# Weight blocks of a transformer layer fetched by several smaller DMAs instead of one

## The chip, the cores and the metric

The kernel runs on one core of a Trainium2 chip. The metric is device time in microseconds (us) from the start to the end of one execution; lower is better. Three executions of the kernel before the change took 1088.27, 1091.22 and 1091.68 us, so the median is 1091.22 us. Another execution was recorded by the hardware profiler: it took 1091.97 us, of which the span from the first to the last instruction is 1090.2 us.

Names used below: TensorE (PE in the profile, with its weight loads as PEld) multiplies matrices, ScalarE (ACT) applies functions, VectorE (DVE) does elementwise work, GpSimd (POOL) a few small operations, and SyncE (SP) issues every DMA of this kernel. SBUF is the on-chip memory, with 128 partitions; PSUM takes the results of TensorE; HBM is the main memory, where inputs, weights and output lie.

## What is computed

One pre-norm transformer layer on a sequence of 2048 rows with 1024 features, in bf16: attention with 32 heads of 32 features, then a feed-forward block with 3584 hidden units.

```python
x = A_x                                       # (1, 2048, 1024)
q, k, v = split(layernorm(x) @ A_wqkv)        # (1024, 3072), 32 heads of 32
p = softmax(q @ k.T * 32**-0.5)               # per head, 2048 x 2048
h = x + concat(p @ v) @ A_wo                  # (1024, 1024)
g = gelu(layernorm(h) @ B_w1 + B_b1)          # (1024, 3584)
out = h + g @ B_w2 + B_b2                     # (3584, 1024)
```

The weights don't fit into the SBUF beside the attention's data, so the weights of the second half (`A_wo`, `B_w1`, `B_w2`, and part of `A_wqkv`) are fetched again for every stretch of 256 rows.

## The kernel before

**Work.** The 2048 rows are cut into eight units of 256 rows. For each unit and each group of four heads, attention makes scores on TensorE (`Att.qk`, matmuls at line 784), takes their exponentials on ScalarE (line 795, tiles `PT` of 128 x 1024), multiplies them with V on TensorE (`Job.pv`, line 821) and sums them with a matmul against ones (`Job.den`, line 850, after a pairwise addition on VectorE at line 836). Between these, as TensorE work of lower priority, come the projection and feed-forward matmuls, made by `mm` (lines 539 to 554): line 546 is a matmul split over four column tiles, lines 549 and 552 the same matmul whole.

**Loops.** After the keys, values and the first queries are made, the loop at line 1133 runs over the units u = 0 to 5: output projection of the next unit (`wo`, line 902), half of the second feed-forward matmul (`ffn2`, line 987), the norm (`ln2`, line 930), the other half of `ffn2`, the first feed-forward matmul of the next unit (`ffn1`, line 943), and the attention of unit u + 3. Units 6 and 7 follow in a tail.

**Weight blocks.** `ffn1` needs 14 blocks of `B_w1` for a unit, `wo` needs 4 blocks of `A_wo`, and `late_q` (line 691) fetches blocks of `A_wqkv` for the later queries. All of these come from `wblock` (line 897): a block is 1024 rows x 256 columns, 512 KB, laid down as 128 partitions with eight runs of 512 bytes each. They go around a ring of four buffers `a_w1r` (line 484), and for the last unit through fourteen buffers `b_w1r` (line 489). `ffn2` needs seven blocks of `B_w2` for each half of a unit (line 994): 512 rows x 512 columns, also 512 KB, as 128 partitions with four runs of 1 KB. Their ring `a_w2r` has seven buffers, and `b_w2r` seven more for the end. Each block was one DMA, hence one instruction on SP, at line 570 inside `dma`.

**Order.** The kernel is written as a graph of tasks (`Graph`). `schedule` (line 109) plays the graph through once at build time with assumed durations and so fixes the order of the instructions on each engine. For a DMA it assumes that SP is taken for `dma_issue` = 0.06 us, that bytes flow at 280 GB/s one DMA behind the other, and a fixed latency (lines 178 to 191). Its result is only an order: on the chip every engine runs its own list in that order, and waits where a semaphore tells it to. A DMA task belongs to one of 24 lanes, each with a semaphore of its own; a DMA adds 16 to it when it has landed, and who needs the data waits for the total that `assign` (line 242) works out. A new task on a lane waits for the one before. SP also waits, before it issues a block, until the matmuls that read the old block in that buffer are done; everything behind it in SP's list waits too. That list also holds the loads of queries (`QT`), residual rows (`hch`), the transposes of the normed rows (`hnT`, line 575) and the stores of the output.

**Emission.** `emit` (line 318) writes for each task its waits, its instructions (`t.fns`, a list) and one semaphore increment on the last of them.

Of the kernel before, what the change touches and what calls it, by code (L numbers as in the profile page):

```python
# [10 lines left out]
E = mybir.EngineType  # L11

P = 128
# [47 lines left out]
class Graph:  # L61
# [47 lines left out]
    def schedule(self, pick_pe, pool, switch=0.104, dma_rate=280.0, dma_lat=2.1, dma_issue=0.06):  # L109
# [5 lines left out]
        free = {e: 0.0 for e in self.ENGS}  # L115
# [5 lines left out]
        n = 0  # L121
# [19 lines left out]
        while n < total:  # L141
            if not events:
                raise RuntimeError("schedule: stuck")
            now = heapq.heappop(events)
            while events and events[0] <= now + 1e-9:
                heapq.heappop(events)
            for e in self.ENGS:
                while free[e] <= now + 1e-9:
                    up = upcoming[e]
                    rd = ready[e]  # L150
                    while up and up[0][0] <= now + 1e-9:
                        rd.append(heapq.heappop(up)[2])
                    if not rd:
                        break
                    if e == E.PE:
                        t = pick_pe(rd, now, state, free_banks(now))
                    else:
                        t = min(rd, key=lambda x: (x.prio, num[x]))
                        if up and t.prio > 0:

                            for (rt, _, u) in up[:6]:
                                if u.prio < t.prio and rt < now + 0.6 * t.occ:
                                    t = None
                                    break
                    if t is None:
                        break
                    rd.remove(t)
                    if t.acq is not None:
                        b = min([x for x in free_banks(now) if x in t.acq.banks], key=lambda x: max([y.done for y in pool[x]], default=0.0))
                        t.deps.update(pool[b])  # L170
                        t.acq.n = b
                        pool[b] = t.acq
                    start = now
                    if e == E.PE:
                        if state["mode"] != t.mode:
                            start += switch
                        state["mode"] = t.mode
                    t.order = len(seqs[e])
                    seqs[e].append(t)
                    if e == E.SP:  # L180
                        k = min(range(self.n_lanes), key=lambda i: lanes[i].done if lanes[i] else 0.0)
                        if lanes[k] is not None:
                            t.deps.add(lanes[k])
                            start = max(start, lanes[k].done)
                        lanes[k] = t
                        t.lane = k
                        free[e] = start + dma_issue
                        s0 = max(state["dma"], start + 0.9)
                        state["dma"] = s0 + t.bytes / dma_rate / 1e3
                        t.done = max(state["dma"], s0) + dma_lat - 0.9  # L190
                    else:
                        free[e] = start + t.occ
                        t.done = start + t.occ + t.lat
                    if t.rel is not None:
                        t.rel.rel.append(t)
                        if len(t.rel.rel) == t.rel.nrel:
                            pool[t.rel.n] = t.rel.rel
                        heapq.heappush(events, t.done)
                    heapq.heappush(events, free[e])
                    n += 1  # L200
                    for s in t.succ:
                        s.left -= 1
                        if s.left == 0:
                            release(s)
# [20 lines left out]
    def assign(self, flows, lane_flows):  # L225

        for t in self.tasks:
            best = {}
            keep = set()
            for d in t.deps:  # L230
                if d.eng == E.SP:
                    keep.add(d)
                elif d.eng != t.eng or t.eng != E.PE:
                    b = best.get(d.eng)
                    if b is None or d.order > b.order:
                        best[d.eng] = d
            t.deps = keep | set(best.values())
            for d in t.deps:
                d.inc = True
        lane_n = [0] * len(lane_flows)  # L240
        for e in self.ENGS:
            c = 0
            for t in self.seqs[e]:
                if e == E.SP:
                    lane_n[t.lane] += 1
                    t.inc = True
                    t.flow = ("L", t.lane)
                    t.value = 16 * lane_n[t.lane]
                else:
                    t.flow = ("E", e)  # L250
                    if t.inc:
                        c += 1
                    t.value = c

        clock = {}
        topo = self._topo()
        last = {}
        for t in topo:
            e = t.eng
            prev = last.get(e)  # L260
            base = dict(prev) if prev else {}
            waits = {}
            for d in t.deps:
                if base.get(d.flow, 0) >= d.value:
                    continue
                if waits.get(d.flow, (0, None))[0] < d.value:
                    waits[d.flow] = (d.value, d)

            keep = dict(waits)
            for f, (v, d) in waits.items():  # L270
                for g, (v2, d2) in waits.items():
                    if g != f and g in keep and clock[d2].get(f, 0) >= v:
                        keep.pop(f, None)
                        break
            t.waits = [(f, v) for f, (v, d) in keep.items()]
            for f, (v, d) in waits.items():
                for k, x in clock[d].items():
                    if base.get(k, 0) < x:
                        base[k] = x
                if base.get(f, 0) < v:  # L280
                    base[f] = v
            last[e] = base
            if t.inc:
                c = dict(base)
                if e != E.SP:
                    c[t.flow] = t.value
                else:
                    c[t.flow] = t.value
                clock[t] = c
        self.sems = {}  # L290
        for e, s in flows.items():
            self.sems[("E", e)] = s
        for i, s in enumerate(lane_flows):
            self.sems[("L", i)] = s
# [23 lines left out]
    def emit(self, e, obj):  # L318
        for t in self.seqs[e]:
            for f, v in t.waits:  # L320
                obj.wait_ge(self.sems[f], v)
            ins = None
            for fn in t.fns:
                ins = fn(obj)
            if t.inc:
                ins.then_inc(self.sems[t.flow], 16 if e == E.SP else 1)


def build_kernel(nc, A_x, A_wqkv, A_wo, B_w1, B_b1, B_w2, B_b2, out):
# [7 lines left out]
    DC = D // P  # L337
# [9 lines left out]
    gr = Graph(N_LANES)  # L347
# [217 lines left out]
    def dma(out_ap, in_ap, nbytes, reads=(), writes=(), prio=0, noncontig=False, after=()):  # L565
        def fn(s):
            if noncontig:
                with nc.allow_non_contiguous_dma(reason="strided gather"):
                    return s.dma_start(out_ap, in_ap)
            return s.dma_start(out_ap, in_ap)  # L570
        return gr.add(E.SP, fn, 0.06, 0.0, reads, writes, prio, nbytes=nbytes, after=after)


    def dma_transpose(out_ap, in_ap, nbytes, reads, writes, prio):
# [5 lines left out]
         reads=[B_ident], writes=[B_ident])  # L580
# [315 lines left out]

    def wblock(R, src_ap, prio=1):
        s = R.next("w1", R.nw1)
        dma(R.w1[:, s, :, :], src_ap.rearrange("(dc p) c -> p dc c", p=P), P * DC * 512, writes=[R.B_w1[s]], prio=prio)
        return s  # L900

    def wo(u, tail=False):
# [84 lines left out]
    def ffn2(u, j, wide=False, W=None, banks=None):  # L987
        R = R2 if wide else R1
        W = W or R1
        c = slice(512 * j, 512 * j + 512)  # L990
        ws = []
        for q in range(FC // 4):
            s = W.next("w2", W.nw2)
            dma(W.w2[:, s, :, :], B_w2[512 * q:512 * q + 512, c].rearrange("(f p) c -> p f c", p=P),
                P * 4096, writes=[W.B_w2[s]], prio=1)
            ws.append(s)
        for t in range(2):
            bank = banks[t] if banks and banks[t] is not None else slot()
# [3 lines left out]
            for fc in range(FC):  # L1002
                s = ws[fc // 4]
# [20 lines left out]
    for k in range(80):  # L1024
        pe(lambda p: p.matmul(psum[:, 6, 0:256], ident[:, :], b2t[:, 0:256], start=True, stop=True), 0.18 if k < 42 else 0.115,  # L1025
           reads=[B_ident, B_b2t], writes=[B_ps[6]], kind="warm")
# [21 lines left out]
    for hc in range(8):  # L1048
# [6 lines left out]
        for k, r in [(k, hc) for k in range(min(hc, NLJ))] + ([(hc, r) for r in range(hc + 1)] if hc < NLJ else []):  # L1055
            n = 8 * k + r
            s = NR + 15 if n == 0 else n - 1 if n < 9 else n
# [220 lines left out]
```

## Time and profile before

| what | value |
|---|---|
| median of three runs | 1091.22 us (1088.27 to 1091.68) |
| profiled execution, of which span | 1091.97 us, 1090.2 us |
| TensorE busy, weight loads beside it | 1045.6 us, 609.6 us |
| ScalarE, VectorE, GpSimd busy | 1014.5, 755.9, 43.4 us |
| mean granted TensorE clock | 0.994 |
| 16 DMA engines, mean over the span | 54.1% for the kernel's own queue, 163 GB/s |
| DMAs: `a_w2r`, `a_w1r` (B_w1), `a_w1r` (A_wo), `b_w1r`, `a_w1r` (A_wqkv), `b_w2r` | 105, 98, 32, 14, 11 and 7 of 512 KB |
| median from issue to landing, in that order | 5.7, 4.4, 4.2, 6.1, 5.0 and 6.6 us |

How to read it: a busy share says how much of the time an engine had an instruction in hand, so two engines over 90% leave little that can be gained by moving work. The DMA share counts the time that packets took on the 16 DMA engines, and the time to landing counts from SP's issue to the last semaphore update. SP itself isn't in the list of busy engines: its instructions issue or wait.

### The profile page before, as it was taken

What the parts mean: (1) busy time and instruction counts of PE and PEld (TensorE: products, weight loads), DVE (VectorE), ACT (ScalarE), POOL (GpSimd) and SP (SyncE); (2) the same over time, 40 slices, a digit from 0 to 9 for tenths busy, and PEclk for the clock granted to TensorE, in tenths of its full rate; (3) what the DMA queues carried; (4) which work ended last, traced back from release to release, by engine and by line L of the source; (5) the groups of instructions that cost most, each with busy time, mean ns of one, the idle gap of its engine ahead of it and who ended that gap; (6) DMA issues with size and microseconds to landing.
All of it is one profiled execution on the core that took longest, in us unless ns stands there. A gap on an engine that the chain in (4) does not pass through costs nothing.

```text
span 1090.2 us, 41817 instructions
## 1 busy us (share of the span) xinstructions
PE 1045.6 (96%) x19048; PEld 609.6 (56%) x19107; DVE 755.9 (69%) x1453; ACT 1014.5 (93%) x1116; POOL 43.4 (4%) x110
## 2 busy tenths in 40 slices
PE   8989999998899999999999999999999999999998
PEld 6656555554344664574475457446545754474483
DVE  7886666666576896599489659948974967696401
ACT  4989999999999999999999999999999999999650
POOL 3200000000010001001000100100010000000100
PEclk9999999999999999999999999999999999899999
DMA  7640010008464667665685766567586656987370
GB/s 194 199 123 11 14 41 3 2 3 287 142 167 133 183 180 209 210 189 154 209 251 157 220 215 189 155 217 233 142 239 205 182 179 160 308 236 228 96 246 20
DMA packets 280146, 178.03 MB, mean 163 GB/s; under 512 B 42656, under 2 KB 274976, under 8 KB 279200
## 3 DMA queue, kind: packets, MB, share of 16 engines
q1 hardware_dynamic: 279968, 175.35, 54.1%
q8 instruction: 150, 2.46, 0.9%
q14 instruction: 28, 0.23, 0.1%
HBM read 161.16 MB, written 10.49 MB: 157 GB/s over the span
## 4 chain that ended last, share of the span: by engine, by line
PE 54%; ACT 39%; DVE 5%; issue 1%; DMA 1%; SPq 0%; POOL 0%; POOLq 0%; DVEq 0%
ACT PT L795 35%; PE ps L549 18%; PE ps L546 12%; PE ps L784 8%; PE ps L821 6%; PE ps L552 5%; PE ps L850 3%; ACT PX L795 2%; DVE PS L836 2%; ACT uu L983 2%; DMA xrb<-in_A_x_dram 0%; DVE OD L866 0%; PE ps L1025 0%; SPq L570 0%; DVE OD L873 0%
## 5 line engine op out<-in xcount | busy, mean ns | idle before, releaser
L795 ACT ACTIVATE PT<-ps 128x1024 bf16<-128x1024 f32 x992 | 922.4, 1082 | 14.7 <-PE ps L784 14.3
L836 DVE TENSOR_TENSOR PS<-PT 128x1024 bf16<-128x1024 bf16 x434 | 286.6, 685 | 128.9 <-PE ps L850 68.1
L784 PE MATMUL ps<-QT,KT 32*128 32x256 bf16 x4096 | 205.3, 274 | 10.7 <-ACT PT L795 5.4
L821 PE MATMUL ps<-PT,V 128*32 128x256 bf16 x3968 | 174.4, 274 | 2.8 <-ACT PT L795 2.8
L784 PEld LDWEIGHTS ps<-QT,KT 32*128 32x128 bf16 x4096 | 61.2, 92 | 166.3 <-ACT PT L795 134.8
L850 PE MATMUL ps<-PS,ones 128*32 128x256 bf16 x1792 | 124.6, 275 | 4.8 <-DVE PS L836 4.0
L821 PEld LDWEIGHTS ps<-PT,V 128*32 128x32 bf16 x3968 | 102.1, 97 | 29.4 <-issue 6.8
L549 PE MATMUL ps<-hnT,a_w1r 128*128 128x256 bf16 x949 | 116.5, 274 | 1.1 <-DVE gT L961 0.5
L549 PEld LDWEIGHTS ps<-hnT,a_w1r 128*128 128x128 bf16 x949 | 87.9, 98 | 25.8 <-issue 14.5
L546 PE MATMUL ps<-a_w2r,gT 128*32 128x512 bf16 x1372 | 98.3, 381 | 0.4 <-DVE hch L1007 0.2
L549 PE MATMUL ps<-a_w2r,gT 128*128 128x512 bf16 x382 | 93.8, 380 | 4.2 <-issue 2.9
L546 PE MATMUL ps<-hnT,a_w1r 128*32 128x256 bf16 x2476 | 88.9, 274 | 4.0 <-issue 1.6
L961 DVE TENSOR_TENSOR gT<-ps,b1f 128x512 bf16<-128x512 f32 x98 | 67.2, 686 | 17.5 <-PE ps L546 9.3
L546 PEld LDWEIGHTS ps<-hnT,a_w1r 128*32 128x32 bf16 x2476 | 60.4, 96 | 20.6 <-issue 16.8
L1007 DVE SCALAR_TENSOR_TENSOR hch<-ps,hch 128x512 bf16<-128x512 f32 x32 | 21.9, 685 | 69.9 <-PE ps L552 47.1
L850 PEld LDWEIGHTS ps<-PS,ones 128*32 128x32 bf16 x1792 | 47.0, 96 | 30.7 <-DVE PS L836 14.2
L549 PEld LDWEIGHTS ps<-a_w2r,gT 128*128 128x128 bf16 x413 | 35.2, 98 | 47.4 <-issue 13.4
L549 PE MATMUL ps<-xnT,Wall 128*128 128x512 bf16 (+1 forms) x256 | 53.5, 344 | 4.5 <-DVE rr L876 2.8
L983 ACT ACTIVATE uu<-uu 128x1024 bf16<-128x1024 bf16 x49 | 53.9, 1108 | 0.0
L546 PEld LDWEIGHTS ps<-a_w2r,gT 128*32 128x32 bf16 x1372 | 30.0, 96 | 25.6 <-issue 14.0
L603 POOL CAST mvb<-mv 128x2 bf16<-128x2 f32 (+1 forms) x25 | 4.9, 201 | 987.2 <-DVE mv L600 987.2
L549 PE MATMUL ps<-Wall,xnT 128*128 128x128 bf16 (+1 forms) x443 | 43.9, 247 | 0.0
(89 smaller groups left out, 1007.9 us busy)
## 6 DMA issues: line engine op xcount, KB each, us to landing
a_w2r<-in_B_w_dram SPq DMA_DIRECT2D x105, 512.0 KB, 5.7
a_w1r<-in_B_w_dram SPq DMA_DIRECT2D x98, 512.0 KB, 4.4
a_w1r<-in_A_wo_dram SPq DMA_DIRECT2D x32, 512.0 KB, 4.2
b_w1r<-in_B_w_dram SPq DMA_DIRECT2D x14, 512.0 KB, 6.1
a_w1r<-in_A_wqkv_dram SPq DMA_DIRECT2D x11, 512.0 KB, 5.0
Wall<-in_A_wqkv_dram SPq DMA_DIRECT2D x17, 256.0 KB, 4.7
xrb<-in_A_x_dram SPq DMA_DIRECT2D x16, 256.0 KB, 4.0
hch<-in_A_x_dram SPq DMA_DIRECT2D x16, 256.0 KB, 5.2
```

The costliest lines, as they stand in the source:

```text
L546: fns.append(lambda p, j=j: p.matmul(psum[32 * j:32 * j + 32, bi(bank), c0:c1], lhsT[:, 32 * j:32 * j + 32], rhs, start=start, stop=stop, ...
L549: t.whole = lambda p: p.matmul(psum[:, bi(bank), c0:c1], lhsT, rhs, start=start, stop=stop, skip_group_check=True)
L552: t = pe(lambda p: p.matmul(psum[:, bi(bank), c0:c1], lhsT, rhs, start=start, stop=stop), occ, reads=reads, writes=[bb(bank)], mode="full" ...
L603: pool(lambda g: g.tensor_copy(mvb[:, sl, :], mv_l[:, sl, :]), 0.25, reads=B_mv[sl], writes=B_mvb[sl], prio=prio)
L784: return p.matmul(psum[:, 2 * us[h // 2] + h % 2, 256 * i:256 * i + 256], KT[32 * h:32 * h + 32, g, k0:k0 + P], QT[32 * h:32 * h + 32, qs, :],
L795: act(lambda a, u=u, k=k: a.activation(PTs[s][:, k, :, :], psum[:, 2 * u:2 * u + 2, :], ACT.Exp, bias=0.0, scale=SCALE), 1024, reads=[B_ps ...
L821: fns.append(lambda p, i=i, h=h: p.matmul(psum[32 * h:32 * h + 32, bi(bank), 0:256], V[:, g, 2 * r + i, 32 * h:32 * h + 32], PTs[s][:, h / ...
L836: dve(lambda v: v.tensor_tensor(PS[:, n, :, :], pairs[:, :, 0:256], pairs[:, :, 256:512], ALU.add), c_dve(1024, 2), reads=B_PTs[s], writes ...
L850: fns.append(lambda p, h=h, rhs=rhs, i=i: p.matmul(psum[32 * h:32 * h + 32, bi(bank), 256:512], ones32[:, :], rhs, start=False, stop=last, ...
L961: t = dve(lambda v: v.tensor_tensor(g[:, fc:fc + 2, :], psum[:, bi(bank), :].rearrange("p (f c) -> p f c", f=2), b1f[:, fc:fc + 2].unsquee ...
L983: act(lambda a: a.activation(w, w, ACT.Tanh, bias=0.0, scale=KT2), 1024, reads=[B_uu[i]], writes=[B_uu[i]], prio=-1)
L1007: drop(dve(lambda v, hs=hs, bank=bank, half=half: v.scalar_tensor_tensor(hch[:, hs, c], psum[:, bi(bank), :], half, hch[:, hs, c], ALU.mul ...
```

## The change

A weight block is now fetched by several DMAs that each cover some of the partitions: four of 32 partitions for the blocks of `wblock` (`B_w1`, `A_wo`, late `A_wqkv`), two of 64 partitions for the blocks of `B_w2`. The pieces of one block are one task of the graph, with one list of waits ahead of the first piece; each piece adds 16 to the same lane's semaphore, so a reader waits for 64 or 32 more than before the block instead of 16 more. The bytes, the length of the runs and the buffers stay as they were. The planner counts SP as taken for 0.06 us for every piece; its bytes and latency are unchanged. All other DMAs stay single.

```diff
@@ schedule
-                        free[e] = start + dma_issue
+                        free[e] = start + dma_issue * len(t.fns)
@@ assign
-                    lane_n[t.lane] += 1
+                    lane_n[t.lane] += len(t.fns)
@@ emit
             for fn in t.fns:
                 ins = fn(obj)
+                if e == E.SP and fn is not t.fns[-1]:
+                    ins.then_inc(self.sems[t.flow], 16)
             if t.inc:
                 ins.then_inc(self.sems[t.flow], 16 if e == E.SP else 1)
@@ build_kernel
+    def dma_pieces(piece, nbytes, n, reads=(), writes=(), prio=0):
+        w = P // n
+        fns = [lambda s, a=a: s.dma_start(*piece(slice(a, a + w))) for a in range(0, P, w)]
+        return gr.add(E.SP, fns, 0.06 * n, 0.0, reads, writes, prio, nbytes=nbytes)
@@ wblock
-        dma(R.w1[:, s, :, :], src_ap.rearrange("(dc p) c -> p dc c", p=P), P * DC * 512, writes=[R.B_w1[s]], prio=prio)
+        src = src_ap.rearrange("(dc p) c -> p dc c", p=P)
+        dma_pieces(lambda q: (R.w1[q, s, :, :], src[q]), P * DC * 512, 4, writes=[R.B_w1[s]], prio=prio)
@@ ffn2
-            dma(W.w2[:, s, :, :], B_w2[512 * q:512 * q + 512, c].rearrange("(f p) c -> p f c", p=P),
-                P * 4096, writes=[W.B_w2[s]], prio=1)
+            src = B_w2[512 * q:512 * q + 512, c].rearrange("(f p) c -> p f c", p=P)
+            dma_pieces(lambda z, s=s, src=src: (W.w2[z, s, :, :], src[z]), P * 4096, 2, writes=[W.B_w2[s]], prio=1)
```

## The prediction

> **What bounds the kernel.** I read the page's busy times first, then the chain that ended last, then the engines' timelines wherever the chain says "issue", and last the DMA views.
>
> ```profile
> PE 1045.6 (96%) x19048; PEld 609.6 (56%) x19107; DVE 755.9 (69%) x1453; ACT 1014.5 (93%) x1116; POOL 43.4 (4%) x110
> ...
> PE 54%; ACT 39%; DVE 5%; issue 1%; DMA 1%; SPq 0%; POOL 0%; POOLq 0%; DVEq 0%
> ...
> L795 ACT ACTIVATE PT<-ps 128x1024 bf16<-128x1024 f32 x992 | 922.4, 1082 | 14.7 <-PE ps L784 14.3
> ```
>
> ScalarE's exponentials and TensorE bound the kernel together; DMA is 1% of the chain, and that lies in the lead. From about 77 to 1020 us ScalarE is the fuller: its whole idle time there is about 8 us. A shorter time to landing can thus bring almost nothing by itself. I paired every weight block's landing with the first weight load that reads it: one late `A_wqkv` block (302.28 us) is met after 0.06 us, one `A_wo` block after 0.84, all 265 others after 1.2 us or more, the typical `B_w1` block after 4 to 5. Weights aren't waited for. What else do the DMAs hold up? The chain near 433 us, and ScalarE's timeline there:
>
> ```profile
> 432.75 0.32 PE ps L784 x5
> 433.08 1.23 issue
> 434.31 0.31 PE ps L784 x3
> ```
>
> ```profile
> 434.64 5.62 ACT L795 ACTIVATE PT<-ps 128x1024 bf16<-128x1024 f32 x6 [1.46 <-PE ps L784]
> ```
>
> TensorE stops for 1.23 us in the midst of eight score matmuls that belong to one task, with nothing to wait for, and ScalarE loses 1.46 us. I followed what could starve it: the instructions themselves.
>
> ```profile
> q1 hardware_dynamic: 279968, 175.35, 54.1%
> q8 instruction: 150, 2.46, 0.9%
> ```
>
> Queue 8 moves 150 packets of 2.46 MB / 150 = 16 KB. TensorE's stream has 19,107 weight loads, as many matmuls and 180 others, 38,394 in all, and 38,394 / 150 = 256: each packet is 256 TensorE instructions. In the records of single packets, six stalls of TensorE without a releaser begin exactly 449 or 450 instructions after 256 times the number of packets that had landed, and end 1.3 to 1.6 us after the next packet's end: 433.08 (1.23 us), 588.64 (0.52), 746.08 (0.60), 764.05 (0.45), 815.83 (1.49) and 863.86 (0.41), 4.70 us together. The ScalarE gaps that follow are 1.46, 0.69, 0.51, 0.73, 1.47 and 0.61, 5.47 us together. So TensorE runs out of instructions.
>
> **Why the fetch is late.** Where DMA is idle (100 to 250 us), the packets start 0.5 to 1.5 us after TensorE passes instruction 168 of its block, the spot that makes this delay most even; I take it as the request. Among weight DMAs the delay is 1 to 4.6 us. It ends at DMA boundaries: with one `a_w1r` block under way the packet starts 0.06 to 0.8 us before that block's landing (2.62 against 2.84 us after the request; 1.97 against 2.39; 1.48 against 1.69). In bursts of `a_w2r` it lets two go by: request at 427.31, blocks landing 2.86, 4.20 and 6.57 us later, packet at 4.56; request at 810.52, blocks at 1.38, 3.66 and 5.00, packet at 4.35. The fetch waits for the rest of the DMA in hand and the whole of the next, not for all queued bytes.
>
> [...]
>
> **The change, part by part.**
>
> *The fetch's wait.* A `B_w1` block gives each of 16 DMA engines 64 packets of 512 B at 27 ns, 1.7 us; a quarter is 0.43 us. A `B_w2` block gives 32 of 1 KB at 46 ns, 1.5 us; a half is 0.74. The wait of up to two DMAs falls from 3.0 to 3.4 us to 0.9 to 1.5 us. The stalls at 433 and 815.83 lie in `B_w2` bursts: the packet comes some 1.5 us earlier, against stalls of 1.23 and 1.49; the other four stalls are under 0.6. I take all six as gone: -4.7 us. Bounds: -5.5 by ScalarE's gaps, 0 if the fetch doesn't profit. What is late next is ScalarE itself: its only other gaps over 0.2 us there (1.03 at 275.8, 0.43 at 291.9, 0.36 at 945.2) end on attention work that the change leaves alone.
>
> *SP's time.* Added are 3 x 155 + 112 = 577 issues, each with its semaphore update.
>
> ```profile
> L570 SPq DMA_DIRECT2D a_w2r<-in_B_w_dram x105: 367/368/2237, 134.5 to 1038.3; - x105
> L570 SPq DMA_DIRECT2D a_w1r<-in_B_w_dram x98: 367/368/1467, 340.3 to 973.0; - x98
> ```
>
> An issue takes 0.37 us; 256 KB loads issued back to back in the lead take 0.43 plus 0.04 between. Four pieces are 0.37 + 3 x 0.47 = 1.8 us, two are 0.84, so SP gains about 577 x 0.47 = 271 us on the 228 it issues now; it mostly waits for buffers. In dense `ffn1` blocks are issued every 2.2 us (359.51, 361.69), in `B_w2` bursts every 1.3 us (421.46, 422.79, 424.04): it fits both. Queued behind the pieces are `QT` loads, used 50 us or more after landing save one before 100 us, and `hnT`, below.
>
> *Landing.* The last quarter is issued 1.4 us after the first. A 64 KB load lands 1.7 to 1.9 us after issue, a 256 KB one 2.6 at best; 128 KB should take about 2.1. That gives 3.5 us against 3.45 to 3.9 for an undivided block alone. Bounds: 0.6 earlier, or 1.4 later if a piece takes as long to land as a block. I take 0, the nearer rows being those of smaller loads; cover is the slack above.
>
> *The crowded stretch.* At 919 to 946 us the DMA engines are full:
>
> ```profile
> 919.00:946.00 27.00, 24.95 (x465) 11.61 (x458) 17.41 (x34) 26.59 (x30) 1.53 (x4) 0.87 1.07 317
> ```
>
> The second `hnT` transpose is issued there at 933.10, 3.3 us after its data were ready, and used 3.43 us after landing. Ahead of it since 919.7 are six blocks of four pieces and four of two: 6 x 1.4 + 4 x 0.47 = 10.3 us more issue time. SP already stands blocked there (issues of 1.67 and 2.24 us), so most of it replaces blocking: I take 0, bound 10.3 - 3.43 = 6.9 us.
>
> *Plan and waits.* No wait is added: a block's waits stand ahead of its first piece as before. In the planner only back-to-back issues shift, by 0.06 to 0.18 us; I take 0.
>
> **Sum.** 1091.97 - 4.7 = 1087.3 for the profiled execution. It lay 0.75 above the median, so for the median 1091.22 - 4.7 = **1086.5**, own range 1083 to 1089.
>
> **Rivals.**
>
> *No gain: 1091.2.* The fetch waits for a fixed number of bytes or packets already queued, whatever DMA they belong to. For: the six stalls all have queued blocks. Waits that end after one `a_w1r` (64 packets on an engine) or two `a_w2r` (also 64) fit this as well. Against: at 972.54 a packet waits past two `a_w1r`-sized blocks (landings at 1.57 and 3.83, packet at 3.90), and the starts sit at boundaries.
>
> *SP late: 1095.* If landings move by the full 1.4 us, the blocks at 302.28, 290.26 and 780.36 (1.27 us of slack) stall for 1.34 + 0.56 + 0.13 = 2.0 us, and `hnT` costs its 6.9: 1086.5 + 8.9 = 1095.4. Against: SP's blocking above.
>
> *Slower pieces: 1120.* This is the case on the other side: a piece that covers a quarter or half of the partitions may move slower than its share. No DMA of this trace covers fewer than 128 partitions, so the factor f is bounded by 1 (a piece takes its share of the time) and 2 (a half takes as long as a whole). Place: the dense `ffn1` phases, where a block is used every 2.2 us; queued `a_w1r` blocks land every 1.5 us (965.2 to 971.3), `a_w2r` every 1.3. It decides from f = 2.2 / 1.5 = 1.47. Above, each of six units loses 18 x (1.5 f - 2.2) + 7 x 1.3 x (f - 1), less some 3.5 of slack: at f = 1.6 5.6 us, six times 34 us, 1086.5 + 34 = 1120; at 2, 120 us. For: the crowded stretch shows that DMA can become the bound. Against: 33% of DMA time is free at 300 to 980 us.
>
> [...]
>
> *It doesn't do what it says:* the waits count all pieces, so this could only be the planner reordering; it is inside "no gain".
>
> **Chances.** Forecast 0.53, no gain 0.17, SP late 0.13, slower pieces 0.17. The last is left out of the range, which runs from 1082.5 to 1100 (SP late with no gain). A difference under 0.3% (3.3 us) can't be told from none here. Faster by more: 0.47 (the forecast up to 1087.9); within: 0.25 (the rest of it 0.06, no gain 0.17, 0.02 of SP late); slower: 0.28 (SP late 0.11, slower pieces 0.17).
>
> **What would show it.** Right: the stalls at instruction 449 vanish, fetch packets start within 2.5 us of the request, SP issues about 1,000 DMAs, landings stay near 4 to 6 us. Wrong: DMA share above 67% at 300 to 980 us or packets longer than 27 and 46 ns (slower pieces); weight loads waiting for `a_w1r` or `hnT` (SP late); the same six stalls (no gain).

## The result and the profile after

The change makes the kernel slower: 1123.87 us (median of six runs, 1121.27 to 1125.26) against 1091.44 us for the kernel before (median of six, 1088.27 to 1097.06). The ratio is 1.0293, 95% interval 1.0264 to 1.0323, or 32.4 us. The profiled execution took 1125.26 us, its span 1123.5 us. One of the five executions of the run e10 below took 1986.44 us, for a reason that no record shows, and is left out of that run's ratio.

The page of the kernel after: busy times, the kernel's own DMA queue, the chain, ScalarE's exponentials (busy us, mean ns of one, idle us ahead of them), and two DMA rows (count, KB each, us to landing).

```profile
PE 1055.2 (94%) x19048; PEld 611.9 (54%) x19107; DVE 756.5 (67%) x1453; ACT 1017.6 (91%) x1116; POOL 43.5 (4%) x110
...
q1 hardware_dynamic: 289200, 175.38, 64.7%
...
PE 55%; ACT 29%; DVE 6%; DMA 5%; issue 3%; SPq 2%; POOL 1%; POOLq 0%; DVEq 0%
...
L804 ACT ACTIVATE PT<-ps 128x1024 bf16<-128x1024 f32 x992 | 923.5, 1070 | 48.1 <-PE ps L793 47.2
...
a_w2r<-in_B_w_dram SPq DMA_DIRECT2D x210, 256.0 KB, 6.2
a_w1r<-in_B_w_dram SPq DMA_DIRECT2D x392, 128.0 KB, 3.0
```

ScalarE does the same work, but its exponentials now stand idle for 48.1 us where it was 14.7, waiting for scores. So it is TensorE that falls behind. The same bytes keep the DMA engines busy for 64.7% of the span, 54.1% before, although only 3% more packets move (289,200 against 279,968). The packets themselves take longer: in the packet records the ones of 1 KB (mostly `B_w2` blocks) take 69.5 ns on average and were at 49.4; those of 512 B (mostly blocks of `wblock`) 32.6 and were at 28.3. In the stretch of the units, TensorE's busy time, its weight loads, VectorE, ScalarE, GpSimd, the clock, the DMA share and GB/s, first of the kernel before, then after:

```profile
300.00:980.00 680.00, 660.75 (x12658) 382.35 (x12689) 517.63 (x995) 673.97 (x732) 22.23 (x56) 0.99 0.67 197
```

```profile
300.00:980.00 680.00, 643.44 (x12102) 366.00 (x12136) 493.67 (x947) 651.84 (x705) 22.30 (x56) 0.98 0.77 185
```

More DMA time (0.77 against 0.67) for fewer bytes in a second (185 against 197 GB/s): this is a slower transfer, not more traffic. What TensorE waits for, total us, times and longest:

```profile
PE ps L548 <- issue: 9.7, 6, 3.1
PE ps L551 <- issue: 9.2, 33, 3.7
PE ps L793 <- issue: 6.2, 4, 2.5
...
PE ps L548 <- DMA a_w1r<-in_B_w_dram: 3.9, 2, 2.4
...
PE ps L551 <- DMA a_w2r<-in_B_w_dram: 2.5, 4, 0.8
```

Two kinds of wait are there. The first is "issue", a stop with nothing to wait for. (Of the 9.2 us in the second row, 3.7 are the wait for `hnT` told below; of the rest, most are short ones, of which the kernel before has 4.6 us in 28.) The chain of waits at 761 us shows the longest, and ScalarE's timeline what it loses there:

```profile
760.58 0.44 PE ps L548 x12
761.02 3.09 issue
764.12 0.41 PE ps L548 x3
```

```profile
766.83 1.02 ACT L804 ACTIVATE PT<-ps 128x1024 bf16<-128x1024 f32 x1 [4.17 <-PE ps L793]
```

Counted as in the prediction (stops that begin at instruction 449 or 450 after the last fetched packet, over 0.2 us), there are 12 of 17.1 us together after and 7 of 4.95 us before (the prediction's six and one of 0.25). The second kind is new, a wait for weights. Here the chain at 534 to 543 us:

```profile
533.98 8.30 DMA a_w2r<-in_B_w_dram
542.29 0.05 issue
542.33 1.04 PE ps L551 x4
```

A half whose issue starts at 533.98 lands 8.3 us later, and a matmul of `ffn2` waits for it. Ten of 105 `B_w2` blocks now land less than 0.3 us before they are used, none before the change. The waits for weights (3.9 + 2.5 + 0.4 us), one of 3.66 us for the transposed rows `hnT` at 965.33 and one of 1.48 at 323.94 (VectorE, which has to free a PSUM bank first, waits for a store of late queries that stands behind pieces in SP's list) make 11.9 us. Only 2.9 of them are for `B_w2` blocks. A third share can't be separated: TensorE's clock was granted at half for 34.1 us of the span, 13.7 before, in pieces of 3.4 us of which several follow a stop (at 664.9 after the one at 662.1; at 763.8 and 866.2, as the ones from 761.0 and 864.1 end). If all of that lay on the path it cost up to 10 us. The sum, 12.1 + 11.9 + at most 10, is about the 32.4 measured, but it is no proof, since parts can overlap. ScalarE's gaps over 0.2 us from 80 us on grew in step, from 7.3 to 38.9 us.

### The profile page after: what moved, and what is told of

Same layout as the page of the kernel before. It is cut to its first block, busy times and chain, and to the rows that moved or that the text cites. A ratio compares the mean times of both kernels' runs of the same rounds, so it can differ in the third digit from the quotient of the medians.

```text
span 1123.5 us, 42394 instructions
## 1 busy us (share of the span) xinstructions
PE 1055.2 (94%) x19048; PEld 611.9 (54%) x19107; DVE 756.5 (67%) x1453; ACT 1017.6 (91%) x1116; POOL 43.5 (4%) x110
## 3 DMA queue, kind: packets, MB, share of 16 engines
q1 hardware_dynamic: 289200, 175.38, 64.7%
q8 instruction: 150, 2.46, 0.9%
## 4 chain that ended last, share of the span: by engine, by line
PE 55%; ACT 29%; DVE 6%; DMA 5%; issue 3%; SPq 2%; POOL 1%; POOLq 0%; DVEq 0%
ACT PT L804 25%; PE ps L551 19%; PE ps L548 13%; PE ps L793 9%; PE ps L830 6%; PE ps L554 5%; PE ps L859 4%; ACT PX L804 2%; DMA a_w2r<-in_B_w_dram 2%; SPq L579 2%; DVE PS L845 2%; ACT uu L993 1%; DMA a_w1r<-in_B_w_dram 1%; DMA q_scratch<-lq 1%; DVE st L607 1%
## 5 line engine op out<-in xcount | busy, mean ns | idle before, releaser
L804 ACT ACTIVATE PT<-ps 128x1024 bf16<-128x1024 f32 x992 | 923.5, 1070 | 48.1 <-PE ps L793 47.2
L793 PE MATMUL ps<-QT,KT 32*128 32x256 bf16 x4096 | 206.3, 275 | 13.7 <-issue 6.2
L548 PE MATMUL ps<-hnT,a_w1r 128*32 128x256 bf16 x2476 | 91.9, 279 | 14.9 <-issue 9.1
L859 PEld LDWEIGHTS ps<-PS,ones 128*32 128x32 bf16 x1792 | 47.8, 97 | 31.9 <-DVE PS L845 13.8
L551 PE MATMUL ps<-xnT,Wall 128*128 128x512 bf16 (+1 forms) x256 | 54.7, 349 | 4.7 <-DVE rr L885 3.0
```

The costliest lines, as they stand in the source:

```text
L548: fns.append(lambda p, j=j: p.matmul(psum[32 * j:32 * j + 32, bi(bank), c0:c1], lhsT[:, 32 * j:32 * j + 32], rhs, start=start, stop=stop, ...
L551: t.whole = lambda p: p.matmul(psum[:, bi(bank), c0:c1], lhsT, rhs, start=start, stop=stop, skip_group_check=True)
L793: return p.matmul(psum[:, 2 * us[h // 2] + h % 2, 256 * i:256 * i + 256], KT[32 * h:32 * h + 32, g, k0:k0 + P], QT[32 * h:32 * h + 32, qs, :],
L804: act(lambda a, u=u, k=k: a.activation(PTs[s][:, k, :, :], psum[:, 2 * u:2 * u + 2, :], ACT.Exp, bias=0.0, scale=SCALE), 1024, reads=[B_ps ...
L859: fns.append(lambda p, h=h, rhs=rhs, i=i: p.matmul(psum[32 * h:32 * h + 32, bi(bank), 256:512], ones32[:, :], rhs, start=False, stop=last, ...
```

## The experiments

Two theories were to be told apart. **Theory A**: which partitions a piece covers sets its speed; slow pieces hold up the instruction fetch and the weights. **Theory B**: the number of pieces is what costs, through SyncE's issue time. All kernels but the two paced ones are edits of the kernel after, and all compute the whole layer.

| kernel | time, us | ratio to before, 95% interval | 512 B, 1 KB packets, ns | own queue | stops at 449: number, us | ScalarE gaps, us |
|---|---|---|---|---|---|---|
| before | 1091.44 | 1 | 28.3, 49.4 | 54.1% | 7, 4.95 | 7.3 |
| after | 1123.87 | 1.0293 (1.0264 to 1.0323) | 32.6, 69.5 | 64.7% | 12, 17.1 | 38.9 |
| e1, W1 pieces only | 1100.95 | 1.0088 (1.0064 to 1.0113) | 32.0, 50.3 | 58.1% | 5, 4.07 | 15.5 |
| e2, W2 pieces only | 1117.18 | 1.0245 (1.0215 to 1.0275) | 28.5, 68.0 | 60.3% | 11, 15.1 | 30.6 |
| e3, all partitions in each piece | 1095.28 | 1.0029 (1.0013 to 1.0045) | 29.0, 50.1 | 55.1% | 5, 2.94 | 12.2 |
| e4, every fourth and second partition | 1126.99 | 1.0317 (1.0278 to 1.0356) | 29.2, 50.1 | 53.6% | 1, 1.88 | 39.3 |
| e5, W2 only, every second partition | 1094.23 | 1.0019 (1.0000 to 1.0037) | 28.3, 50.0 | 54.5% | 4, 4.36 | 8.9 |
| e6, W1 only, all partitions | 1095.30 | 1.0018 (1.0002 to 1.0034) | 28.9, 49.6 | 55.0% | 3, 2.23 | 12.7 |
| e7, before, two W2 blocks queued | 1094.45 | 1.0020 (1.0004 to 1.0036) | 28.2, 52.1 | 54.7% | 8, 4.89 | 11.7 |
| e8, before, one W2 block queued | 1217.52 | 1.1136 (1.1102 to 1.1170) | 28.1, 51.8 | 49.2% | 2, 0.70 | 117.3 |
| e9, e1 in alternate order | 1097.63 | 1.0053 (1.0037 to 1.0069) | 30.2, 50.1 | 56.5% | 6, 3.62 | 13.8 |
| e10, W1 only, in halves | 1103.45 | 1.0108 (1.0072 to 1.0144) | 34.3, 50.8 | 60.6% | 10, 5.01 | 16.0 |

Packets are means over the whole run; "own queue" is queue 1's share of the page; ScalarE's gaps are those over 0.2 us between 80 us and its last exponential. Packets, stops and gaps are of one profiled execution each, so differences of a few stops say little. Each ratio is to executions of the kernel before taken beside that run (medians from 1091.35 to 1093.17 us), and what a run loses in us is worked out from its ratio.

### One part alone (e1, e2)

```diff
 e1, in ffn2: W2 blocks whole again
-dma_pieces(..., P * 4096, 2, writes=[W.B_w2[s]], prio=1)
+dma_pieces(..., P * 4096, 1, writes=[W.B_w2[s]], prio=1)
 e2, in wblock: W1, Wo and Wqkv blocks whole again
-dma_pieces(..., P * DC * 512, 4, writes=[R.B_w1[s]], prio=prio)
+dma_pieces(..., P * DC * 512, 1, writes=[R.B_w1[s]], prio=prio)
```

> Only the blocks of wblock stay cut into four (32 partitions each); the blocks of B_w2 are whole again, so 465 of the 577 added DMAs remain. Theory A (coverage: a piece on 32 or 64 neighbouring partitions moves at about half speed): 1 KB packets are back at 46 ns, queued quarters land every 0.55 us as in the changed kernel, the long fetch stalls in and behind the B_w2 bursts go, and the time is 1097 us (1091 to 1107). Theory B (number of DMAs: each issue and each semaphore update costs): four fifths of the 32 us remain, 1117 us.

> Only the blocks of B_w2 stay cut into two (64 partitions each); the blocks of wblock are whole again, so 112 of the 577 added DMAs remain. Theory A (coverage): queued halves land every 1.1 us, 1 KB packets stay near 71 ns, and most of the loss remains, 1112 us (1103 to 1120). Theory B (number of DMAs): one fifth of the 32 us remains, 1097 us.

The 112 extra issues for W2 cost 26.7 us, the 465 for the other blocks 9.6. That is the wrong way round for theory B. Each edit also slows only its own packets: e2 the 1 KB ones, e1 those of 512 B. On e2's page, though a quarter as many DMAs were added as in e1, the DMA share and ScalarE's idle time are the larger:

```profile
q1 hardware_dynamic: 281760, 175.35, 60.3%
...
L804 ACT ACTIVATE PT<-ps 128x1024 bf16<-128x1024 f32 x992 | 923.6, 1075 | 40.1 <-PE ps L793 39.6
```

### The same pieces over all partitions (e3)

As many DMAs of as many bytes, but a piece is two of the block's runs on every one of the 128 partitions.

```diff
-fns = [lambda s, a=a: s.dma_start(*piece(slice(a, a + w))) for a in range(0, P, w)]
+fns = [lambda s, a=a: s.dma_start(*piece(a)) for a in range(n)]
 wblock
-dma_pieces(lambda q: (R.w1[q, s, :, :], src[q]), ...)
+dma_pieces(lambda q: (R.w1[:, s, 2 * q:2 * q + 2, :], src[:, 2 * q:2 * q + 2, :]), ...)
 ffn2
-dma_pieces(lambda z, s=s, src=src: (W.w2[z, s, :, :], src[z]), ...)
+dma_pieces(lambda z, s=s, src=src: (W.w2[:, s, 2 * z:2 * z + 2, :], src[:, 2 * z:2 * z + 2, :]), ...)
```

> As many pieces of the same bytes as the changed kernel, but each piece covers all 128 partitions and takes only some of the runs (two of eight for wblock, two of four for B_w2). Theory A (coverage): packets are back at 27 and 46 ns, blocks land as before the change, 1091 us if the instruction fetch waits for a fixed number of queued packets (the stalls at instruction 449 stay near 4.7 us), 1086.5 if it waits for DMAs, as predicted (the stalls go). Theory B (number of DMAs): 1124 us as the changed kernel.

```profile
q1 hardware_dynamic: 289200, 175.38, 55.1%
...
L804 ACT ACTIVATE PT<-ps 128x1024 bf16<-128x1024 f32 x992 | 922.9, 1082 | 23.0 <-PE ps L793 22.0
```

The count of packets is that of the kernel after to the last one, and their time is back near that of before. Of the 2.9% all but 0.3% is gone. But this kernel isn't faster than before either, and that speaks on the prediction's own step: here the pieces move at full speed, so a fetch that waits for the DMA in hand and the next one would have been early. The packet requested at 434.26 us starts 4.33 us later, past five or six landings of halves; the one requested at 533.03 after 4.10 us, past six. The fetch doesn't count DMAs. Counted from the records, as packets that start on one DMA engine (the mean of 16) between the request and the fetch, the longest waits in W2 bursts pass 88 before, 96 in e3 and 114 after; in W1 bursts it is 133 before and 161 after. Whether the blocks are whole (before) or in halves at full speed (e3), about as much work goes ahead of the fetch. So it is what is queued that counts, and cutting it into more DMAs doesn't shorten it. That the number is fixed isn't shown.

### Strided partitions (e4, e5)

Again 32 or 64 partitions in each piece, no longer neighbours: every fourth for the blocks of `wblock`, every second for W2. In e5 the blocks of `wblock` stay whole.

```diff
-fns = [lambda s, a=a: s.dma_start(*piece(slice(a, a + w))) for a in range(0, P, w)]
+fns = [lambda s, a=a: s.dma_start(*piece(slice(a, P, n))) for a in range(n)]
```

> As many pieces and as many partitions in each as in the changed kernel, but every fourth partition (wblock) or every second (B_w2) instead of neighbours. Theory A, if it matters which partitions (neighbours share a way into SBUF): packets near 27 and 46 ns and a time like that of the pieces over all partitions, 1088 to 1094 us. If it is the number of partitions in a DMA that sets its speed: 1 KB packets near 71 ns and 1124 us. Theory B (number of DMAs): 1124 us with short packets.

> Blocks of wblock whole; blocks of B_w2 in two halves that take every second partition. Beside the run with halves of 64 neighbours (1117 us) only the choice of partitions differs, and SP needs as long for a piece (0.62 us). Theory A (neighbouring partitions slow the packets): 1 KB packets at 46 ns, fetch stalls at instruction 449 back to some 5 us, 1092 to 1098 us. Rival S (SP's longer issue of the halves is what costs): 1113 to 1120 us.

e5 against e2 is the pair that decides: as many DMAs of the same bytes, partitions and runs, and the same time on SyncE. First e2's row of issues (min, median, max ns), then e5's:

```profile
L579 SPq DMA_DIRECT2D a_w2r<-in_B_w_dram x210: 595/616/3728, 135.1 to 1066.0; - x105
```

```profile
L579 SPq DMA_DIRECT2D a_w2r<-in_B_w_dram x210: 601/616/2337, 133.1 to 1042.4; - x105
```

With a median of 616 ns in both, e2 loses 26.7 us and e5 2.1. On e5's page the DMA share and ScalarE's idle time are near those of before:

```profile
q1 hardware_dynamic: 281760, 175.35, 54.5%
...
L804 ACT ACTIVATE PT<-ps 128x1024 bf16<-128x1024 f32 x992 | 921.9, 1071 | 16.6 <-PE ps L793 15.8
```

The 14 halves of the W2 burst near 425 us land over 15.0 us in e2 (427.96 to 443.00) and 11.9 us in e5 (425.87 to 437.75). It is the choice of neighbours that costs. How much, the traces of before and after show: halves of neighbours that queue land every 1.10 us (eight from 429.20 to 436.91, after), 256 KB in 1.10 us or 238 GB/s, and queued blocks before every 1.33 us (430.18 to 431.51), 394 GB/s, a ratio of 0.60. Why, no run shows: that neighbours share a way into the SBUF, as the expectations of e4 and e9 have it, is a supposition.

e4 missed its expected time and is the slowest of the cut versions, with packets at full speed and hardly a stop at 449. Its rows of issues and of waits show why:

```profile
L579 SPq DMA_DIRECT2D a_w1r<-in_B_w_dram x392: 598/614/1954, 349.5 to 1013.6; - x196
```

```profile
PE ps L551 <- DMA a_w1r<-in_B_w_dram: 5.8, 4, 3.4
...
PE ps L551 <- DMA a_w1r<-in_A_wo_dram: 4.6, 2, 2.8
PE ps L548 <- DMA a_w1r<-in_B_w_dram: 4.5, 3, 2.5
```

A strided quarter takes SyncE 0.61 us to issue, a quarter of neighbours 0.45. Four take 4 x 0.61 + 3 x 0.04 = 2.6 us, more than the 2.2 us in which `ffn1` uses a block, so weights come late because they are issued late: TensorE's waits for weight blocks are 19.4 us in e4, and its wait for `hnT` at 962.10 is 5.5, of the 35 us lost. No run takes the issue time alone out of e4, so this is read from its waits. Theory B's cost is real; it is not what slowed the change.

### The W1 pieces (e6, e9, e10)

e6 is e3 with W2 blocks whole; e9 is e1 with the quarters issued in the order of partitions 0, 64, 32, 96; e10 is e1 with two halves of 64 neighbours.

```diff
 e9
-fns = [... for a in range(0, P, w)]
+fns = [... for a in sorted(range(0, P, w), key=lambda a: a % 64)]
 e10, in wblock
-dma_pieces(..., P * DC * 512, 4, writes=[R.B_w1[s]], prio=prio)
+dma_pieces(..., P * DC * 512, 2, writes=[R.B_w1[s]], prio=prio)
```

> Blocks of B_w2 whole; blocks of wblock in four pieces of all 128 partitions (two of eight runs each). Beside the run with quarters of 32 neighbours (1101 us) only the coverage differs; SP needs 0.47 us for a piece against 0.45. Theory A: 1092 to 1095 us, hnT or late blocks cost what is left. Rival S (four issues of SP per block cost): 1099 to 1103 us.

> W1, Wo and late Wqkv in four quarters as in the run with these alone (1100.95 us, 1.0088 times before; 512-byte packets 32 ns on average), but issued in the order of partitions 0, 64, 32, 96; W2 blocks whole. Theory A, that a transfer of neighbouring partitions has few ways into the SBUF and that two queued neighbours share the same ones: pieces that follow each other now lie in different halves of the partitions, so if the engines work on two pieces at once the packets come back towards 27 to 29 ns and the time to 1094 to 1097 us. Rival: all engines go through one piece at a time, in step, so that the neighbour in the queue makes no difference: packets 32 ns, 1099 to 1103 us.

> W1, Wo and late Wqkv in two halves of 64 neighbouring partitions each, W2 blocks whole. SyncE issues 2 x 0.62 us for a block instead of 4 x 0.45. Theory A, that the partitions which a piece covers set its rate, and that 64 neighbours are as badly off as 32: packets of 512 bytes stay longer than the 28.3 ns of before, 31 ns or more, and the time is 1097 to 1106 us. Rival: the rate goes by the number of partitions in a transfer, so that 64 are better off than 32: packets 28 to 30 ns and 1093 to 1096 us.

e6 sets apart SyncE's share: 465 extra issues at full packet speed cost 0.18%, some 2 us (0.2 to 3.7 by the interval). The rest of e1's 9.6 us goes with the partitions. e10 follows theory A: fewer issues than e1, yet packets of 34.3 ns and no less time. e9 lies between its two forecasts, at 30.2 ns and 1097.63 us. That fits pieces that overlap in part when they follow each other in different halves of the partitions, but no view shows the overlap itself, and the intervals of e9 and e1 touch. Where e6's 2 us go can be seen near 945 us, where ScalarE loses 0.35 us before and 2.08 us in e6 (timelines of before and of e6):

```profile
945.52 6.52 ACT L795 ACTIVATE PT<-ps 128x1024 bf16<-128x1024 f32 x7 [0.35 <-PE ps L784]
```

```profile
952.07 1.94 ACT L804 ACTIVATE PT<-ps 128x1024 bf16<-128x1024 f32 x2 [2.08 <-PE ps L793]
```

The transpose of `hnT` stands behind the crowd of pieces in SP's list, is issued at 942.02 in place of 933.10 us, and a weight load waits for it.

### Fewer queued blocks (e7, e8)

If the fetch waits for what is queued, a shorter queue should help the kernel before. A W2 block there waits for the landing of the second-last W2 block (e7) or of the last one (e8). Order and DMAs are unchanged.

```diff
 e7 (e8 with w2s[1:] in place of w2s[2:])
+w2s.append(dma(W.w2[:, s, :, :], ...))
 ...
+w2s.sort(key=lambda t: t.order)
+for t, old in zip(w2s[2:], w2s):
+    t.deps.add(old)
```

> The kernel before with one wait more: a B_w2 block is issued only when the second last B_w2 block has landed; the planned order of every engine is the same. Theory Q (the instruction fetch waits for packets that are already queued on its DMA engine): with at most two B_w2 blocks under way the fetch starts at most 0.8 + 2 x 1.3 = 3.4 us after the request instead of 4.6, the two long stalls in the bursts at 433 and 816 us fall from 1.2 and 1.5 to under 0.4 us, the four short ones of B_w1 stay: 1089.5 us (1088 to 1091). If the fetch waits for something else: 1091 to 1093 us and the same stalls.

> As the run before, but a B_w2 block waits until the last one has landed, so only one is under way. Theory Q: in the bursts the fetch starts within 2.2 us and no stall at instruction 449 is left there; but a block now takes 3.6 us or more from issue to landing instead of 1.3 between two, seven take 25 us against some 19 us until the last is used, so the matmuls wait for B_w2: about 5 us for each of six units, 1120 us (1110 to 1140). If the fetch waits for something else, the stalls stay as they were, on top of that.

The stops that were aimed at went both times, and the gain stayed away. In e7 the stops in the W2 bursts, at 433 and 816 us before, are gone, but others grew (1.35 us at 671.71, 0.73 at 749.78, 0.58 at 866.90), and their sum is what it was, 4.89 us; the matmuls also wait 1.6 us for W2 blocks now. In e8 the fetch starts within 3.85 us and 0.70 us of stops are left, while the matmuls wait for the blocks, more than forecast:

```profile
PE ps L549 <- DMA a_w2r<-in_B_w_dram: 36.4, 21, 2.5
PE ps L549 <- DMA a_w1r<-in_B_w_dram: 32.2, 5, 7.2
```

No version was found that beats the kernel before.

## Why the prediction was wrong

**The step that failed** is the one headed *The fetch's wait*: "a quarter is 0.43 us ... a half is 0.74". It gave a piece its share of the block's packet time. The usual 1 KB packet (the median) took 71 ns and not 46, and halves in a burst landed every 1.10 us, so a block took 2.2 us and not 1.3. Instead of 4.7 us gained there are 12.1 us more of stops. The price of this was worked out in the rival *Slower pieces*, at 1120 us, and given 0.17. Its cause holds, by e2 against e5, and so do its signs (DMA share 0.77, longer packets). Its total came within 4 us, but by luck and not by its formula. Put in f = 1.65 for W2 (2.20 / 1.33 us a block, by landings). For W1 f is 1.15 by packet time (32.6 / 28.3) and 1.47 by landings (four queued quarters in 2.2 us, a queued block before in 1.5, both at the lower quartile), so W1 doesn't pass its threshold of 1.47 by either. That leaves 7 x 1.3 x 0.65 = 5.9 a unit, less 3.5 of slack: 2.4, or 14 us for six units, all of it for W2. Waits for data were 11.9, with 2.9 for W2 blocks among them. What the rival left out, that slow transfers lengthen the fetch's wait too, made 12.1, and the clock may have made the rest. The prediction's argument against it, a third of DMA time free, was a mean over 680 us, and W2 blocks come in bursts: from 429.2 to 436.9 us, where a half lands every 1.10 us, the DMA share is 1.11, so the engines are full.

**The rule for the fetch** failed as well, and that by itself would have taken the gain away. "The rest of the DMA in hand and the whole of the next" doesn't survive e3, where a fetch waits past five or six DMAs. The rival *No gain* was nearer: it is what is already queued that counts, whatever DMA it belongs to, though the number of packets isn't shown to be fixed (88 to 161 in the longest waits). No gain and a little of *SP late* are what e3 and e6 show, both at 1095. That starts sat at DMA boundaries was no argument between the two: in e3 the packet requested at 434.26 us starts 0.12 us after a landing too, but after the sixth. What ends the fetch's wait is not settled.

**What bounds the kernel** was right: in all kernels the lost time shows as gaps of ScalarE. So was the reading of the six stops as missing instructions (they begin at the same instruction number in all kernels). **Plan and waits** was right too: the order of every engine's tasks is the same before and after.

**SP's time.** Quarters were put at 1.8 us and take 4 x 0.45 + 3 x 0.04 = 1.9. Halves were put at 0.84 and take 2 x 0.62 + 0.04 = 1.27, just inside the 1.3 us of a W2 burst. The row of 128-partition loads was not the right one for 64 partitions. It changed little: e5 has that cost in full and loses 2.1 us.

**Landing** was taken as unchanged for quarters, with 1.4 us as the upper bound: from the first issue to the last landing a `B_w1` block went from 4.4 to 5.0 us. W2 blocks were not priced there at all. They went from 5.7 to 7.5, and those of `b_w2r` from 6.6 to 12.0.

**The crowded stretch** was taken as 0 with a bound of 6.9 us. TensorE waits 3.66 us for `hnT` at 965.33 after, 0.96 in e3 at 947.27, 1.66 in e6 at 947.92. "Most of it replaces blocking" was right for SyncE's part, by e3 and e6; with slow pieces the wait is more than twice as long.

## What to carry to other kernels

A load cut by neighbouring partitions was not the same load in smaller pieces: 1 KB packets took 69.5 ns after and 49.4 before, and 50.1 with as many pieces along the free dimension, each over all partitions (e3). So cut that way, and test for it by the time of single packets, which shows at once whether transfers or their number are to blame. A mean DMA share says nothing of a burst (after, 0.77 over 680 us and 1.11 from 429.2 to 436.9). When instructions starve behind bulk loads, cutting the loads need not help: the longest wait of the fetch was 4.56 us with whole blocks and 4.33 with pieces at full speed (e3).

## What the runs showed of the hardware that was not expected

- **Issue time went with the shape.** On SyncE a DMA of 128 partitions took 0.37 us alone (before) and 0.47 in a row of pieces (e3), one of 32 neighbours 0.31 to 0.45 (after), one of 64 neighbours (after, e10) or of strided partitions (e4, e5) 0.60 to 0.64, from the least to the median of the ring blocks. That half the partitions take longer to issue than all of them was not expected, and no run here says why.
- **Pieces that follow each other in different halves of the partitions were a little faster** (512 B packets 30.2 against 32.0 ns, e9 against e1, or 6% shorter; 1097.63 against 1100.95 us).
- **A fetch of TensorE's instructions started 7.1 us after its request** (833.15 us, after; 4.6 at most before), though queue 8 takes 0.9% of the DMA time: with as little traffic as that, the stops at instruction 449 grew by 12.1 us.
- **The clock was at half after some stops:** half clock for 34.1 us after, 13.7 before, 41.0 in e4, in steps of 3.4 us. After, it follows the stops of 2.25, 3.09 and 2.46 us at 662.14, 761.02 and 864.13, and not those of 1.96 and 2.03 at 466.50 and 834.18. How much of the time that took was not measured by itself.
